# Two attention and feed-forward layers in one decode step: 32 units of K kept instead of 30, and 12 units of streaming room instead of 14

## The chip, the cores and the metric

The kernel runs on one core of a Trainium2 chip. Its time is device microseconds for one launch, the median of three runs: 2575.14 us (2574.99 to 2575.31).

## The reference

Two identical layers (same weights, same K and V caches) are run one after the other on two sequences of one token each, all in float32:

```
x = x + attention(layernorm(x))     # 32 query heads, 8 KV heads, 32768 keys of 128
x = x + geglu(layernorm(x))         # w_gate, w_up 512x1792, w_down 1792x512
x = x + attention(layernorm(x))     # the same K cache, V cache, wq, wo again
x = x + geglu(layernorm(x))
```

`attention` is softmax(q k^T / sqrt(128)) v, then times wo; `geglu` is (gelu(h w_gate) * (h w_up)) w_down. K and V together are 512 MB, and each layer reads all of them.

## The kernel before, in words

**Units and memory.** One unit is 512 float32 columns on 128 partitions, 256 KB. One pair (KV head g, sequence b) has 64 units of K and 64 of V. All that is streamed lies in one tile, `mem`, of 108 units. In the long stretches it holds three pieces of 32 units, K or V, at places 0, 32 and 64; places 96 to 108 hold wo.

**The stream.** Lines 231 to 257 list every transfer in order (wq, K and V of the pairs, wo, then gate and up `gu`, then down `wd`). `pump` issues them on SP's queue in that order; one that has no free place waits and stops all behind it. `done` gives a place back behind the last matmul that reads it, and pumps. So a transfer starts when its place has been read, and it is then queued behind what is still under way. `plan` (line 86) fixes the places of the transfers around the change of layers; the others take the first hole that fits.

**Layer 1 runs the pairs backwards**, so its first pair is the last pair of layer 0. That pair's V (64 units) stays in `mem` and isn't loaded again. Of its K, units 0 to 29 stay in `mem` (`KEPT = 30`: 28 at places 64 to 92, two at 92 and 93), and four more are copied by VectorE and ScalarE into four idle PSUM banks (`stash`, lines 408 to 415) and back later (lines 398 to 403). The other 30 units (34 to 63) are loaded again (`K_PARTS[1]`).

**Between the layers** V and the kept K fill 94 units, and 14 units (places 94 to 108) are left. Through these pass, as a ring of four pieces of 3 to 4 units: `gu` (28 units in 8 pieces), `wd` (14 in 4), wq of layer 1 (32 in 10), the first 14 units of the K that is loaded again. Each is issued when the piece before it at its place has been read. wo of the last head (4 units) is queued between the first and the second piece of the last V and lies at 104; so `gu` piece 3, which takes the same place, is issued only when the last head has been projected (`last_head`, matmuls at line 531).

**The computing chain there**: last V piece (matmuls L457), `combine` (L466, L470, L475), `last_head` (L531), `residual` (L547 to L557), gate and up (L610), gelu, transposed (L584), down (L595 in two pieces, then L531 in two), `residual`, wq (L346), transposed (L358), scores of layer 1 (L386).

Of the kernel before, what the change touches and what calls it, by code (L numbers as in the profile page):

```python
# [16 lines left out]
P = 128  # L17
NB = 2
HKV = 8
REP = 4  # L20
DM = 512
KC = DM // P
DF = 1792
FN = 256
FW = (256, 256, 256, 128)
# [16 lines left out]


K_PARTS = [{ORDER[-1]: [(32, 32), (28, 4), (0, 28)]},
           {ORDER[-1]: [(34, 6), (40, 4), (44, 4), (48, 4), (52, 12)], ORDER[-2]: [(0, 8), (8, 16), (24, 8), (32, 8), (40, 24)]}]

V_SPLIT = [{ORDER[-1]: [32, 16, 8, 4, 4]}, {ORDER[0]: [32, 16, 8, 4, 4]}]


KEPT = 30  # L50
STEPS = [4, 8, 8, 8]


WQ_SPLIT = [[32], [3, 4, 3, 4, 3, 4, 3, 4, 3, 1]]
GU_SPLIT = [[1792, 1792, 1536, 2048], [FH // KC] * KC]
WD_SPLIT = [[3, 4, 3, 4], [3, 4, 4, 2, 1]]

WO_GROUPS = [[(0, 1), (2, 3), (4, 5), (6,), (7,)], [(7,), (6,), (5, 4), (3, 2), (1,), (0,)]]

# [6 lines left out]
def pieces(split):  # L66

    out, s = [], 0
    for n in split:
        out.append((s, n))  # L70
        s += n
    return out
# [13 lines left out]
def plan():  # L86


    last, before = ORDER[-1], ORDER[-2]
    out = {}  # L90

    def put(kind, l, pair, spots):
        for (s, n), o in zip(parts(kind, l, pair), spots):
            out[kind, l, *pair, s] = o

    put("k", 0, before, [32, 0])
    put("v", 0, before, [64, 32])
    put("k", 0, last, [0, SPARE, 64])
    put("v", 0, last, [32, 16, 8, 4, 0])
    out["wo", 0, HKV - 1] = out["wo", 1, HKV - 1] = 104  # L100
    for i in range(8):
        out["gu", 0, i] = [94, 97.5, 101, 104][i % 4]
    for i in range(10):
        out["wd", 0, i] = out["wq", 1, i] = [94, 97, 101, 104][i % 4]
    put("k", 1, last, [98, 104, 94, 64, 68])
    put("k", 1, before, [84, 92, 64, 72, 32])
    put("v", 1, before, [0, 64])
    return out
# [24 lines left out]
def block_kernel(ctx: ExitStack, tc: tile.TileContext, x, consts, kt, vt, wq, wo, won, gu, wd, out):  # L133
# [83 lines left out]
    def flat(src, g, b, s, n):  # L217
        h, c = divmod(s, CHUNK)
        return src[b, g, h, :, c * UNIT:(c + n) * UNIT]

    def add(key, src, rows, cols):
        stream.append((key, src, rows, cols))
# [8 lines left out]
    for l in range(2):  # L231
        for i, (s, m) in enumerate(pieces(WQ_SPLIT[l])):
            add(("wq", l, i), wq[:, s * DM:(s + m) * DM], P, m * DM)
        for n, (g, b) in enumerate(orders[l]):
            second = meets(l, n)[1]
            vp = parts("v", l, (g, b))
            for s, m in parts("k", l, (g, b)):
                add(("k", l, g, b, s), flat(kt, g, b, s, m), P, m * UNIT)
            for s, m in [] if second else vp:
                if n % 2 == 1 and s == vp[1][0]:  # L240
                    group = wo_group(l, g)
                    o = g % 2 * HALF
                    if (l, g) in NARROW:
                        h = NARROW[l, g]
                        add(("won", l, g), won[l, :, :, :h * NSEL * DM], NROW, h * NSEL * DM)
                        add(("wo", l, g), wo[g // 2, :, o + h * DM:o + HALF], P, (REP - h) * DM)
                    elif len(group) == 2 and g == group[0]:
                        add(("wo", l, g), wo[g // 2], P, 2 * HALF)
                    elif len(group) == 1:
                        add(("wo", l, g), wo[g // 2, :, o:o + HALF], P, HALF)  # L250
                add(("v", l, g, b, s), flat(vt, g, b, s, m), P, m * UNIT)
        for e in range(2):
            half_of = gu[e * P * FH:(e + 1) * P * FH].rearrange("(p c) -> p c", p=P)
            for j, (c, m) in enumerate(pieces(GU_SPLIT[l])):
                add(("gu", l, len(GU_SPLIT[l]) * e + j), half_of[:, c:c + m], P, m)
        for j, (o, m) in enumerate(pieces(WD_SPLIT[l])):
            add(("wd", l, j), wd[:, o * DM:(o + m) * DM], P, m * DM)

# [78 lines left out]
    def window(k, v):  # L337
        return xpad[:, 30 + 32 * k - 2 * v:62 + 32 * k - 2 * v]
# [30 lines left out]
    def scores(l, n, g, b):  # L369
        first, second = meets(l, n)  # L370
        mx = wk.tile([P, 2], F32, name="mx", bufs=1)

        todo = [(("k", l, g, b, s), 0, s, m) for s, m in parts("k", l, (g, b))]
        if second:
            own = [(("k", 0, g, b, 0), s, s, m) for s, m in pieces(STEPS)]
            todo = own + [(None, SPARE, KEPT - 2, 2), (None, BACK, KEPT, QUAD)] + todo
        order = [j for key, o, s, m in todo for j in range(s, s + m)]
        for key, o, s, m in todo:
            if key is None:
                w = mem[:, o * UNIT:(o + m) * UNIT].rearrange("p (a c) -> p a c", a=m)  # L380
            else:
                w = get(key, at[key][0][1] if key in at else m)[:, o:o + m, :]
            for j in range(s, s + m):
                u, c, t = j // 32, j // QUAD % 8, j % QUAD
                tile_of = [i for i in order if i // 32 == u and i % QUAD == t]
                nc.tensor.matmul(S[u][32 * t:32 * t + 32, :], qpad[n % 2][:, 28 - 4 * c:60 - 4 * c],  # L386
                                 w[:, j - s, :], start=(j == tile_of[0]), stop=(j == tile_of[-1]))
                if j == [i for i in order if i // 32 == u][-1]:
                    nc.vector.tensor_reduce(mx[:, u:u + 1], S[u], axis=AX.X, op=OP.max)  # L389
            if first and s < KEPT:  # L390
                continue
            if first:

                done(key, 2, m - 2)
            elif key is None:
                give(o, m)
                pump()
            elif second and o + 64 <= BACK < o + m + 64 and key[1] == 0:

                done(key, o, BACK - 64 - o)  # L400
                for bank, i, copy in zip(where, range(QUAD), 2 * [nc.scalar.copy, nc.vector.tensor_copy]):
                    copy(mem[:, (BACK + i) * UNIT:(BACK + i + 1) * UNIT], bank)
                state["full"] = False
            else:
                done(key, o, m)
        return mx

    def stash(g, b):

        places = [SPARE + 2, SPARE + 3, 0, 1]  # L410
        for bank, o, copy in zip(where, places, 2 * [nc.vector.tensor_copy, nc.scalar.copy]):
            copy(bank, mem[:, o * UNIT:(o + 1) * UNIT])
        state["full"] = True
        give(0, 2)
        done(("k", 0, g, b, KEPT - 2), 2, 2)

    def softmax(mx):
        nm = wk.tile([P, 1], F32, name="nm", bufs=1)
# [146 lines left out]
    def feedforward(l):  # L565
# [33 lines left out]

        tops = sum(WD_SPLIT[l][:2])  # L600
        for e in range(2):
            for i, (s, m) in enumerate(pieces(GU_SPLIT[l])):
                key = "gu", l, len(GU_SPLIT[l]) * e + i
                w = flat_of(key)
                c = 0
                for k in range(KC):
                    for t, n in enumerate(FW):
                        if s <= c < s + m:
                            o = both[e][32 * t:32 * t + 32, :].rearrange("p (x c) -> p x c", x=2)[:, :, :n]
                            nc.tensor.matmul(o, window(k, 0), w[:, c - s:c - s + 2 * n].rearrange("p (x c) -> p x c", x=2),  # L610
                                             start=(k == 0), stop=(k == KC - 1))
                        c += 2 * n
                done(key)
                if e == i == 0:
                    spread(A)
                    rstd = state["rstd"]
                    hrr, cube, root = (wk.tile([P, 1], F32, name=n, bufs=1) for n in ("hrr", "cube", "root"))
                    nc.vector.scalar_tensor_tensor(hrr, rstd, 0.5, rstd, op0=OP.mult, op1=OP.mult)
                    nc.vector.tensor_scalar(cube, rstd, math.sqrt(0.044715), None, op0=OP.mult)
                    nc.vector.tensor_scalar(root, rstd, math.sqrt(2.0 / math.pi), None, op0=OP.mult)  # L620
                if e == i == 1:
                    hidden(0)
                if i == len(GU_SPLIT[l]) - 1:
                    gelu(e)
                if e:
                    warm(256, W[:NB])
# [47 lines left out]
def halves(gate, up):  # L674

    out = []
    for e in range(2):
        c, cols = e * DF // 2, []
        for n in FW:
            cols += [gate[:, c:c + n], up[:, c:c + n]]  # L680
            c += n
        w = np.concatenate(cols, axis=1).reshape(KC, P, -1).transpose(1, 0, 2)
        out.append(np.ascontiguousarray(w).reshape(-1))
    return np.concatenate(out)


# [33 lines left out]
```

## Time and profile before

| | |
|---|---|
| median of 3 runs | 2575.14 us |
| the profiled execution | 2575.15 us |
| its span (first to last instruction) | 2573.3 us |
| read from HBM | 1103.71 MB, 429 GB/s over the span |
| TensorE busy, VectorE, ScalarE | 53%, 6%, 3% |
| mean DMA share | 99.5% by queue q1 alone |

Read it from the DMA side: the 16 DMA engines work nearly all the time, and the slices of 64 us that move less than the others are the first, the one around 1300 us (389 GB/s) and the last. The one around 1300 us is the change of layers.

### The profile page before, as it was taken

The numbers are of one execution on the slowest core, as the hardware profiler recorded it, in microseconds if no ns is written. First come the engines' busy times: TensorE is split into PE (matmuls) and PEld (weight loads), VectorE is DVE, ScalarE is ACT, GpSimd is POOL, SyncE is SP. The second block draws the span as 40 slices with busy tenths as digits, with TensorE's granted clock in tenths as the row PEclk, the third lists the DMA queues.
The fourth block names the chain that finished last, engine by engine and source line by source line (L and its number), as shares of the span: only waits on it lengthen the run. The fifth ranks groups of instructions, "written<-read, shape, count | busy, mean of one in ns | idle before, by whom it ended". The sixth has DMA issues, their size and how long they took to land.

```text
span 2573.3 us, 20343 instructions
## 1 busy us (share of the span) xinstructions
PE 1368.5 (53%) x9528; PEld 370.5 (14%) x9528; DVE 143.1 (6%) x482; ACT 80.9 (3%) x187; POOL 2.6 (0%) x10
## 2 busy tenths in 40 slices
PE   3545555445544555564586455454545544554657
PEld 0111111111111111111121111111111111111112
DVE  0000000000000000000011000000000000000001
ACT  0000000000000000000000000000000000000000
POOL 0000000000000000000000000000000000000000
PEclk8777777777777776777798777777777777777779
DMA  9999999999999999999999999999999999999998
GB/s 424 431 432 436 430 431 432 434 432 432 437 427 437 434 426 437 430 431 434 422 389 430 435 434 433 430 434 431 435 430 434 431 433 436 429 436 430 431 435 368
DMA packets 27363, 1105.07 MB, mean 429 GB/s; under 512 B 3184, under 2 KB 3440, under 8 KB 6896
## 3 DMA queue, kind: packets, MB, share of 16 engines
q1 hardware_dynamic: 26992, 1103.70, 99.5%
q8 instruction: 74, 1.21, 0.2%
q10 hardware_dynamic: 288, 0.08, 0.0%
q14 instruction: 9, 0.07, 0.0%
HBM read 1103.71 MB, written 0.07 MB: 429 GB/s over the span
## 4 chain that ended last, share of the span: by engine, by line
DMA 67%; PE 23%; another core or an unknown queue 9%; DVE 1%; ACT 0%; issue 0%; SPq 0%; POOL 0%; ACTq 0%; DVEq 0%
DMA mem<-in_vt 45%; DMA mem<-in_kt 19%; PE A L457 12%; PE S L386 9%; DMA cst<-in_consts 2%; DMA mem<-in_gu 1%; DMA mem<-in_wq 1%; PE W L509 0%; DMA mem<-in_wd 0%; PE M L470 0%; ACT big L466 0%; PE T L432 0%; PE W L491 0%; PE M L346 0%
## 5 line engine op out<-in xcount | busy, mean ns | idle before, releaser
L386 PE MATMUL S<-mem,qpad 128*32 128x512 f32 x4096 | 580.5, 730 | 536.3 <-DMA mem<-in_kt 535.1
L457 PE MATMUL A<-mem,big 128*16 128x512 f32 x4096 | 578.0, 727 | 484.0 <-DMA mem<-in_vt 484.0
L386 PEld LDWEIGHTS S<-mem,qpad 128*32 128x32 f32 x4096 | 146.5, 131 | 957.1 <-issue 512.6
L457 PEld LDWEIGHTS A<-mem,big 128*16 128x16 f32 x4096 | 122.2, 112 | 910.5 <-DMA mem<-in_vt 518.2
L389 DVE TENSOR_REDUCE mx<-S 128x1 f32<-128x512 f32 x64 | 44.3, 692 | 1118.5 <-PE S L386 1118.5
L429 ACT ACTIVATE big<-S,bias 128x512 f32<-128x512 f32 x64 | 43.4, 683 | 1206.6 <-DVE bias L425 1206.6
L432 PE MATMUL T<-cst,big 128*128 128x128 f32 x256 | 50.8, 347 | 39.0 <-ACT big L429 38.7
L475 DVE TENSOR_REDUCE oT<-M 128x4 f32<-128x64 f32 x32 | 7.2, 225 | 1100.6 <-PE M L470 1100.6
L466 ACT ACTIVATE big<-A,linv 128x512 f32<-128x512 f32 (+1 forms) x34 | 22.3, 662 | 1146.9 <-PE A L457 1146.9
L433 DVE COPY big<-T 128x512 f32<-128x512 f32 x64 | 43.8, 691 | 60.8 <-PE T L432 60.8
L432 PEld LDWEIGHTS T<-cst,big 128*128 128x128 f32 x256 | 36.5, 174 | 49.5 <-ACT big L429 49.3
L470 PE MATMUL M<-cst,big 128*128 128x128 f32 x128 | 21.3, 288 | 24.9 <-ACT big L466 24.9
L437 PE MATMUL M<-cst,both 128*128 128x4 f32 x64 | 16.9, 335 | 29.5 <-DVE both L435 29.5
L421 PE MATMUL M<-cst,nm 128*128 128x128 f32 x32 | 10.3, 323 | 34.6 <-DVE nm L419 34.6
L306 PE MATMUL S<-part,cst 128*128 128x128 f32 (+3 forms) x64 | 23.2, 445 | 0.3 <-DVE var L323 0.3
L346 PE MATMUL M<-mem,xpad 128*32 128x512 f32 x128 | 20.1, 637 | 3.9 <-DMA mem<-in_wq 3.4
L470 PEld LDWEIGHTS M<-cst,big 128*128 128x128 f32 x128 | 13.4, 140 | 53.2 <-ACT big L466 53.2
L437 PEld LDWEIGHTS M<-cst,both 128*128 128x128 f32 x64 | 14.1, 275 | 39.4 <-DVE both L435 39.4
L509 PE MATMUL W<-mem,oT 128*2 128x512 f32 x96 | 12.5, 592 | 3.8 <-DVE oT L475 3.8
L421 PEld LDWEIGHTS M<-cst,nm 128*128 128x128 f32 x32 | 4.3, 133 | 63.9 <-DVE nm L419 63.9
L610 PE MATMUL A<-mem,xpad 128*32 128x512 f32 (+1 forms) x64 | 10.2, 623 | 5.5 <-DMA mem<-in_gu 4.3
L491 PE MATMUL W<-mem,big 16*2 16x512 f32 x80 | 12.6, 784 | 0.6 <-DVE big L486 0.6
(100 smaller groups left out, 162.9 us busy)
## 6 DMA issues: line engine op xcount, KB each, us to landing
mem<-in_gu SPq DMA_DIRECT2D x12, 896.0 KB, 24.5
mem<-in_wo SPq DMA_DIRECT2D x5, 2048.0 KB, 53.5
mem<-in_vt SPq DMA_DIRECT2D x2, 4096.0 KB, 42.9
mem<-in_kt SPq DMA_DIRECT2D x1, 7168.0 KB, 49.8
mem<-in_kt SPq DMA_DIRECT2D x3, 2048.0 KB, 16.1
mem<-in_kt SPq DMA_DIRECT2D x1, 6144.0 KB
mem<-in_kt SPq DMA_DIRECT2D x4, 1024.0 KB, 7.7
mem<-in_wo SPq DMA_DIRECT2D x4, 1024.0 KB, 51.0
```

What stands on the lines that cost most here:

```text
L306: nc.tensor.matmul(bank, ident[:, :bank.shape[0]], part.to_broadcast([P, n]), start=True, stop=True)
L346: nc.tensor.matmul(qp[32 * t:32 * t + 32, :], window(k, v), w[:, i - s, :], start=(i < 4), stop=(i >= 8 * KC - 4))
L386: nc.tensor.matmul(S[u][32 * t:32 * t + 32, :], qpad[n % 2][:, 28 - 4 * c:60 - 4 * c], w[:, j - s, :], start=(j == tile_of[0]), stop=(j == ...
L389: nc.vector.tensor_reduce(mx[:, u:u + 1], S[u], axis=AX.X, op=OP.max)
L421: nc.tensor.transpose(m[:, :P], nm.to_broadcast([P, P]), ident)
L429: nc.scalar.activation(p[u], S[u], AF.Exp, bias=bias, scale=SCALE, accum_out=ls[:, u:u + 1])
L432: nc.tensor.transpose(T[u][:, k * P:(k + 1) * P], p[u][:, k * P:(k + 1) * P], ident)
L433: nc.vector.tensor_copy(p[u], T[u])
L437: nc.tensor.matmul(m[:, :REP], both.to_broadcast([P, P]), same, start=True, stop=True)
L457: nc.tensor.matmul(A[32 * t:32 * t + 16, :], p[u][:, at_p:at_p + 16], w[:, QUAD * i + t, :], start=(j == 0), stop=(j == NU // QUAD - 1))
L466: nc.scalar.activation(md[:, i:i + 512 // n], A[:, i:i + 512 // n], AF.Copy, scale=linv)
L470: nc.tensor.transpose(m[:, c * P:(c + 1) * P], md[:, c * P:(c + 1) * P], ident)
```

## The change

Of the last pair's K, 32 units stay in `mem` (places 64 to 96) and units 32 to 35 go through the PSUM banks, so that 28 units (36 to 63) are loaded again instead of 30. For what streams between the layers 12 units are left (places 96 to 108) instead of 14. The pieces become 4 units, some 3 or 2: `gu` 4, 4, 4, 2 and 2, 4, 4, 4 (in both layers; the blocks of a piece are now listed in `GU_PARTS`, the weights lie in HBM in that order, and the matmuls follow it), `wd` of layer 0 3, 4, 4, 3, wq of layer 1 eight times 4, and the K that is loaded again 4, 4, 4, 4, 4, 8. wo of layer 0's last head is queued behind all of the last V, at place 96.

```diff
-           {ORDER[-1]: [(34, 6), (40, 4), (44, 4), (48, 4), (52, 12)], ORDER[-2]: ...
+           {ORDER[-1]: [(36, 4), (40, 4), (44, 4), (48, 4), (52, 4), (56, 8)], ORDER[-2]: ...
-KEPT = 30
-STEPS = [4, 8, 8, 8]
-WQ_SPLIT = [[32], [3, 4, 3, 4, 3, 4, 3, 4, 3, 1]]
-GU_SPLIT = [[1792, 1792, 1536, 2048], [FH // KC] * KC]
+KEPT = 32
+STEPS = [4, 4, 4, 8, 8]
+WQ_SPLIT = [[32], [4] * 8]
+GU_SPLIT = [[2 * sum(FW[t] for k, t in part) for part in parts] for parts in GU_PARTS]
...
-    out["wo", 0, HKV - 1] = out["wo", 1, HKV - 1] = 104
+    out["wo", 0, HKV - 1], out["wo", 1, HKV - 1] = 96, 104
-        out["gu", 0, i] = [94, 97.5, 101, 104][i % 4]
+        out["gu", 0, i] = [100, 104, 96, 100, 102, 104, 96, 100][i]
+        out["wq", 1, i] = [96, 100, 104][i % 3]
+        out["wd", 0, i] = [104, 96, 100, 104][i]
...
-                if n % 2 == 1 and s == vp[1][0]:
+                if n % 2 == 1 and s == vp[1][0] and not meets(l, n)[0]:
...
+            if meets(l, n)[0]:
+                add(("wo", l, g), wo[g // 2, :, g % 2 * HALF:(g % 2 + 1) * HALF], P, HALF)
...
-        places = [SPARE + 2, SPARE + 3, 0, 1]
-        for bank, o, copy in zip(where, places, 2 * [nc.vector.tensor_copy, nc.scalar.copy]):
-            copy(bank, mem[:, o * UNIT:(o + 1) * UNIT])
+        for i, bank, copy in zip(range(QUAD), where, 2 * [nc.vector.tensor_copy, nc.scalar.copy]):
+            copy(bank, mem[:, i * UNIT:(i + 1) * UNIT])
```

SP's queue from the last V of layer 0 (`in_vt` of 16384 columns, then 8192, 4096 and twice 2048) to its `wd`; a unit is 512 columns. Before:

```order
L196 DMA mem<-in_vt 128x16384
L196 DMA mem<-in_wo 128x2048
L196 DMA mem<-in_vt 128x8192
L196 DMA mem<-in_vt 128x4096
L196 DMA mem<-in_vt 128x2048 x2
L196 DMA mem<-in_gu 128x1792 x2
L196 DMA mem<-in_gu 128x1536
L196 DMA mem<-in_gu 128x2048
```

and now:

```order
L203 DMA mem<-in_vt 128x16384
L203 DMA mem<-in_vt 128x8192
L203 DMA mem<-in_vt 128x4096
L203 DMA mem<-in_vt 128x2048 x2
L203 DMA mem<-in_wo 128x2048
L203 DMA mem<-in_gu 128x2048 x3
L203 DMA mem<-in_gu 128x1024 x2
L203 DMA mem<-in_gu 128x2048 x3
```

wo has moved behind the last V piece. Behind that piece there was room for three `gu` pieces, 10.5 units; now there is room for wo and two `gu` pieces, 12 units.

SP's queue from `wd` of layer 0 to the end of the K that layer 1's first pair loads again. Before:

```order
L196 DMA mem<-in_wd 128x1536
L196 DMA mem<-in_wd 128x2048
L196 DMA mem<-in_wq 128x1536
L196 DMA mem<-in_wq 128x512
L196 DMA mem<-in_kt 128x3072
L196 DMA mem<-in_kt 128x2048 x3
L196 DMA mem<-in_kt 128x6144
```

(of `wd` and wq, which alternate 1536 and 2048, two rows each are shown), and now:

```order
L203 DMA mem<-in_wd 128x1536
L203 DMA mem<-in_wd 128x2048 x2
L203 DMA mem<-in_wd 128x1536
L203 DMA mem<-in_wq 128x2048 x8
L203 DMA mem<-in_kt 128x2048 x5
L203 DMA mem<-in_kt 128x4096 x2
```

Ten wq pieces have become eight; of the K, 30 units have become 28 (the last 4096 row belongs to the next pair).

PE's matmuls on the first `gu` half of layer 0. Before:

```order
L610 MATMUL S_87<-mem,xpad 32x512 x3
L610 MATMUL S_87<-mem,xpad 32x2x128
L321 MATMUL A<-sq,part 128x8
L610 MATMUL S_87<-mem,xpad 32x512 x3
L610 MATMUL S_87<-mem,xpad 32x2x128
L610 MATMUL S_87<-mem,xpad 32x512 x3
L610 MATMUL S_87<-mem,xpad 32x2x128
```

and now:

```order
L620 MATMUL S_87<-mem,xpad 32x512 x3
L620 MATMUL S_87<-mem,xpad 32x2x128 x2
L331 MATMUL A<-sq,part 128x8
L620 MATMUL S_87<-mem,xpad 32x512 x6
L620 MATMUL S_87<-mem,xpad 32x2x128 x2
L620 MATMUL S_87<-mem,xpad 32x512 x3
```

The same 16 matmuls of a half, 12 of 512 columns and 4 of 256, stand in another order; a piece has five, four or two of them instead of four.

## Rows read from the trace of the kernel before

**Rows 1.** Page, whole span: its parts 1 to 4
```profile
span 2573.3 us, 20343 instructions
PE 1368.5 (53%) x9528; PEld 370.5 (14%) x9528; DVE 143.1 (6%) x482; ACT 80.9 (3%) x187; POOL 2.6 (0%) x10
...
q1 hardware_dynamic: 26992, 1103.70, 99.5%
q8 instruction: 74, 1.21, 0.2%
...
DMA 67%; PE 23%; another core or an unknown queue 9%; DVE 1%; ACT 0%; issue 0%; SPq 0%; POOL 0%; ACTq 0%; DVEq 0%
```

**Rows 2.** Stretches: busy us (count) by engine, PEclk, DMA share, GB/s
```profile
100.00:1200.00 1100.00, 570.86 (x3910) 150.75 (x3910) 55.61 (x183) 30.49 (x71) 0.00 (x0) 0.73 1.00 432
1285.00:1294.00 9.00, 8.29 (x78) 3.70 (x76) 0.67 (x5) 1.21 (x4) 0.00 (x0) 1.00 0.70 272
1298.00:1302.00 4.00, 1.78 (x10) 0.45 (x10) 1.57 (x4) 0.96 (x2) 0.00 (x0) 0.83 0.95 329
1302.00:1336.00 34.00, 28.14 (x211) 9.20 (x212) 3.03 (x12) 1.95 (x5) 0.55 (x1) 0.97 1.02 420
1336.00:1346.00 10.00, 9.14 (x68) 2.87 (x66) 1.39 (x5) 1.66 (x3) 0.00 (x0) 1.00 1.00 402
1346.00:1360.00 14.00, 7.81 (x68) 2.15 (x64) 1.05 (x2) 0.10 (x1) 0.00 (x0) 0.83 1.02 420
```

**Rows 3.** Chain that ended last, around the last V: start us, us, what
```profile
1261.13 26.88 DMA mem<-in_vt
...
1288.06 1.10 PE A L457 x8
...
1290.82 1.10 PE W L531 x32
...
1291.94 4.81 DMA mem<-in_gu
...
1296.79 1.12 PE S L610 x7
...
1297.92 8.82 DMA mem<-in_gu
```

**Rows 4.** Timeline of SP, 1260 us and 1294 us: start, us, what is issued
```profile
1261.55 30.71 SPq L196 DMA_DIRECT2D mem<-in_gu  x4
1294.36 3.89 SPq L196 DMA_DIRECT2D mem<-in_gu  x4
```

**Rows 5.** Timeline of PE: start, us, out<-in, count, [idle before, releaser]
```profile
1293.24 1.06 PE L610 MATMUL S<-mem,xpad 128*32 128x512 f32 x8
...
1300.22 1.57 PE L610 MATMUL A<-mem,xpad 128*32 128x512 f32 x8 [2.36 <-DMA mem<-in_gu]
...
1306.78 1.07 PE L610 MATMUL A<-mem,xpad 128*32 128x256 f32 x10 [0.34 <-DMA mem<-in_gu]
...
1311.53 1.04 PE L595 MATMUL W<-mem,big 128*2 128x512 f32 x8
...
1333.83 1.07 PE L346 MATMUL M<-mem,xpad 128*32 128x512 f32 x8 [0.80 <-DMA mem<-in_wq]
...
1340.51 4.93 PE L386 MATMUL S<-mem,qpad 128*32 128x512 f32 x44 [0.65 <-DVE qpad L367]
```

**Rows 6.** Copies into the idle banks, line 412: duration ns, first and last start
```profile
L412 ACT COPY T<-mem x1: 590/590/590, 1258.3 to 1258.3; 128x512 f32<-128x512 f32 x1
...
L412 DVE COPY T<-mem x1: 685/685/685, 1260.4 to 1260.4; 128x512 f32<-128x512 f32 x1
```

**Rows 7.** Chain that ended last, the end of the kernel
```profile
2543.72 17.39 DMA mem<-in_gu
...
2561.16 1.11 PE A L610 x2
...
2570.38 0.29 DVE big L562
```

More of the change, by code (lines that the diff above doesn't have):

```diff
@@ L44 @@
 K_PARTS = [{ORDER[-1]: [(32, 32), (28, 4), (0, 28)]},
-           {ORDER[-1]: [(34, 6), (40, 4), (44, 4), (48, 4), (52, 12)], ORDER[-2]: [(0, 8), (8, 16), (24, 8), (32, 8), (40, 24)]}]
+           {ORDER[-1]: [(36, 4), (40, 4), (44, 4), (48, 4), (52, 4), (56, 8)],
+            ORDER[-2]: [(0, 8), (8, 16), (24, 8), (32, 8), (40, 24)]}]
 V_SPLIT = [{ORDER[-1]: [32, 16, 8, 4, 4]}, {ORDER[0]: [32, 16, 8, 4, 4]}]
-KEPT = 30
-STEPS = [4, 8, 8, 8]
-WQ_SPLIT = [[32], [3, 4, 3, 4, 3, 4, 3, 4, 3, 1]]
-GU_SPLIT = [[1792, 1792, 1536, 2048], [FH // KC] * KC]
-WD_SPLIT = [[3, 4, 3, 4], [3, 4, 4, 2, 1]]
+KEPT = 32
+STEPS = [4, 4, 4, 8, 8]
+WQ_SPLIT = [[32], [4] * 8]
+WD_SPLIT = [[3, 4, 4, 3], [3, 4, 4, 2, 1]]
+GU_PARTS = [[[(0, 0), (0, 1), (0, 2), (0, 3), (1, 3)], [(1, 0), (1, 1), (1, 2), (2, 0)],
[3 rows of a table added]
+GU_SPLIT = [[2 * sum(FW[t] for k, t in part) for part in parts] for parts in GU_PARTS]
 WO_GROUPS = [[(0, 1), (2, 3), (4, 5), (6,), (7,)], [(7,), (6,), (5, 4), (3, 2), (1,), (0,)]]
@@ L99, in plan @@
     put("v", 0, last, [32, 16, 8, 4, 0])
-    out["wo", 0, HKV - 1] = out["wo", 1, HKV - 1] = 104
+    out["wo", 0, HKV - 1], out["wo", 1, HKV - 1] = 96, 104
     for i in range(8):
-        out["gu", 0, i] = [94, 97.5, 101, 104][i % 4]
-    for i in range(10):
-        out["wd", 0, i] = out["wq", 1, i] = [94, 97, 101, 104][i % 4]
-    put("k", 1, last, [98, 104, 94, 64, 68])
+        out["gu", 0, i] = [100, 104, 96, 100, 102, 104, 96, 100][i]
+        out["wq", 1, i] = [96, 100, 104][i % 3]
+    for i in range(4):
+        out["wd", 0, i] = [104, 96, 100, 104][i]
+    put("k", 1, last, [104, 96, 100, 64, 68, 72])
     put("k", 1, before, [84, 92, 64, 72, 32])
@@ L251, in block_kernel @@
                 add(("v", l, g, b, s), flat(vt, g, b, s, m), P, m * UNIT)
+            if meets(l, n)[0]:
+                add(("wo", l, g), wo[g // 2, :, g % 2 * HALF:(g % 2 + 1) * HALF], P, HALF)
         for e in range(2):
             half_of = gu[e * P * FH:(e + 1) * P * FH].rearrange("(p c) -> p c", p=P)
-            for j, (c, m) in enumerate(pieces(GU_SPLIT[l])):
-                add(("gu", l, len(GU_SPLIT[l]) * e + j), half_of[:, c:c + m], P, m)
+            for j, (c, m) in enumerate(pieces(GU_SPLIT[e])):
+                add(("gu", l, len(GU_SPLIT[0]) * e + j), half_of[:, c:c + m], P, m)
         for j, (o, m) in enumerate(pieces(WD_SPLIT[l])):
@@ L375, in scores @@
             own = [(("k", 0, g, b, 0), s, s, m) for s, m in pieces(STEPS)]
-            todo = own + [(None, SPARE, KEPT - 2, 2), (None, BACK, KEPT, QUAD)] + todo
+            todo = own + [(None, SPARE, KEPT - QUAD, QUAD), (None, BACK, KEPT, QUAD)] + todo
         order = [j for key, o, s, m in todo for j in range(s, s + m)]
@@ L392, in scores @@
             if first:
-                done(key, 2, m - 2)
+                done(key, QUAD, m - QUAD)
             elif key is None:
@@ L408, in stash @@
     def stash(g, b):
-        places = [SPARE + 2, SPARE + 3, 0, 1]
-        for bank, o, copy in zip(where, places, 2 * [nc.vector.tensor_copy, nc.scalar.copy]):
-            copy(bank, mem[:, o * UNIT:(o + 1) * UNIT])
+        for i, bank, copy in zip(range(QUAD), where, 2 * [nc.vector.tensor_copy, nc.scalar.copy]):
+            copy(bank, mem[:, i * UNIT:(i + 1) * UNIT])
         state["full"] = True
-        give(0, 2)
-        done(("k", 0, g, b, KEPT - 2), 2, 2)
+        give(0, QUAD)
+        pump()
     def softmax(mx):
@@ L601, in feedforward @@
         for e in range(2):
-            for i, (s, m) in enumerate(pieces(GU_SPLIT[l])):
-                key = "gu", l, len(GU_SPLIT[l]) * e + i
+            order = [t for part in GU_PARTS[e] for k, t in part]
+            at_t = 0
+            for i, part in enumerate(GU_PARTS[e]):
+                key = "gu", l, len(GU_PARTS[e]) * e + i
                 w = flat_of(key)
                 c = 0
[L606 to L612, printed above, removed]
+                for k, t in part:
+                    n = FW[t]
+                    o = both[e][32 * t:32 * t + 32, :].rearrange("p (x c) -> p x c", x=2)[:, :, :n]
+                    nc.tensor.matmul(o, window(k, 0), w[:, c:c + 2 * n].rearrange("p (x c) -> p x c", x=2),
+                                     start=(t not in order[:at_t]), stop=(t not in order[at_t + 1:]))
+                    at_t += 1
+                    c += 2 * n
                 done(key)
@@ L622, in feedforward @@
                     hidden(0)
-                if i == len(GU_SPLIT[l]) - 1:
+                if i == len(GU_PARTS[e]) - 1:
                     gelu(e)
@@ L676, in halves @@
     out = []
[L677 to L683, printed above, removed]
+    for e, parts in enumerate(GU_PARTS):
+        cols = []
+        for k, t in sum(parts, []):
+            c = e * DF // 2 + sum(FW[:t])
+            cols += [w[k * P:(k + 1) * P, c:c + FW[t]] for w in (gate, up)]
+        out.append(np.ascontiguousarray(np.concatenate(cols, axis=1)).reshape(-1))
     return np.concatenate(out)
```

3 rows, old and new, of the table GU_PARTS are left out of this document.

## The prediction, written before the changed kernel ran

> **What bounds the kernel now.** The page comes first: TensorE is busy 53% of the span, one DMA queue 99.5%, and the chain that ended last is 67% DMA [rows 1]. In the long stretches data flows at 432 GB/s [rows 2], so a unit of 262,144 bytes takes 0.607 us. Then the stretches around the change of layers: the flow falls to 272 GB/s for 9 us, to 329 for 4 us, and stays at 420 and 402 while the small pieces pass [rows 2]. In work at 432 GB/s that is 9 x (1 - 272/432) = 3.3 us, 0.95 us, 0.9 us and 0.7 us. So a change can gain by moving fewer bytes, or by closing these dips.
>
> Then the chain of waits, to see which dips count. The last V piece landed at 1261.13 + 26.88 = 1288.01; the last head's projection (L531) began 2.81 us behind that and ended 3.9 behind it; it freed the place of gu piece 3, which was issued at 1291.94 and landed at 1296.75 [rows 3]. Between the two landings lie 14.5 units (10.5 that were queued, and these 4). At the full rate they take 8.80 us, and they took 8.74. So the DMA engine that lagged most never ran empty in the 3.3 us dip: what was idle there were engines that had got ahead. As a landing waits for the last engine, this dip cost little by itself. The second dip did cost: piece 4, issued at 1294.36 [rows 4], let its matmuls start at 1300.22 [rows 5]. Its 3.5 units took 3.4 us behind piece 3 instead of 2.1, a loss of 1.3 us.
>
> **Two units less.** 30 units of K loaded again become 28: 2 x 0.607 = -1.21 us, since the stream is the chain before and behind this place. This is the firmest term.
>
> **wo behind V, and 12 units queued in place of 10.5.** V lands 4 units (2.43 us) earlier in the stream, wo 2.43 us behind it. The projection isn't ready to use wo until 2.81 us behind V, so the new wait on wo has 0.4 us in hand. If that were gone, PE's queue behind it (a warming matmul, the residual's, the first gu piece) would come as much later, and the refill that the projection issues with it. The refill is issued 3.9 us behind V as before, with 12 x 0.607 = 7.3 us queued instead of 6.4. I count nothing for this dip alone, by the landings above; 0 to -3.3 us is possible.
>
> **The second dip.** How soon does an issued piece start to land? Piece 3 took 4.81 us for 4 units (2.43), so the lead was 2.38 us [rows 3]. Piece 4 was issued 6.35 us behind V with 14.5 units ahead (8.80 us): 8.80 - 6.35 - 2.38 leaves 0.07 us in hand, and it was late. Now the pieces in its role are the two of 2 units; they wait for the first gu piece, whose matmuls ran from 5.23 to 6.3 us behind V (1293.24 to 1294.3 [rows 5]). Ahead of them lie wo and three pieces, 16 units or 9.7 us: 1.0 us in hand. Of the 1.3 us I take -0.9, as the refills behind are spaced about as before; the bounds are 0 and -1.3.
>
> **A ring of 12 units instead of 14.** When a piece has been read, 8 units are under way in place of about 10.5: 4.86 us instead of 6.4. The reading takes 1.1 us (a wq piece: 1.07 [rows 5]), the lead 2.38: 1.4 us in hand, before 2.9. It is tightest at the first wq piece. It now waits for down's second piece, read until 1311.53 + 1.04 [rows 5], 5.83 us behind the landing of the last gu piece (1297.92 + 8.82 [rows 3]). Under way behind that landing is then only wd, 14 units or 8.50 us: 8.50 - 5.83 - 2.38 = 0.3 us in hand. Before, a wq piece of 3 stood in between, and the piece that waited there had 2.1 us. I cost it at nothing while the 0.3 us hold. The largest lead of the rows is piece 4's, 5.86 - 2.12 = 3.7 us; with that the place would lose 1.1 us, which is the upper end. The lower end is -0.3 us, a third of the 0.9 us that the small pieces lose now, as 3 and 3.5 units grow to 4.
>
> **The K that is loaded again.** Up to the 48th unit its pieces wait for wq reads, those behind for scores. The scores start at 1340.51 [rows 5] in either kernel, and the pieces at 64 and above free as before. The one of 12 becomes 4 and 8, with 20 units ahead of the 8 instead of 18 ahead of the 12, while the piece before has 12 ahead instead of 14. I take 0, within 0.7 us either way (what 402 GB/s lost).
>
> **Copies into the banks.** Four before and four after, on the same engines, the last one from 1260.4 on for 0.69 us [rows 6]. The V piece that waits for them landed 26.88 us after its issue though its own data are 2.4 us, so over 20 us of queued transfers hide it. 0.
>
> **The end.** From the landing of the last gu piece at 2561.12 to the last copy at 2570.38 the chain is computing [rows 7], and wd lies beside it. The last piece now has five matmuls instead of four, two of them in one strip and of half width: 0 to a quarter of the 1.1 us they took, I take +0.1. As the data behind that piece are the same 14 units, this chain moves with the stream and neither hides nor adds to the gain.
>
> **Sum.** -1.21 - 0.9 + 0 + 0 + 0.1 = -2.0 us. The profiled execution took 2575.15 us (span 2573.3 and 1.85 around it), the median of the runs is 2575.14. So 2573.1 us, and 2572.0 to 2574.2 if the forecast's mechanism is right.
>
> **A rule that speaks against the change.** The small pieces of the ring moved at 420 GB/s against 432 [rows 2], 3% less. The Trainium skill ("DMA: Bandwidth & Descriptors", Bandwidth) asks for transfers of 1 MiB or more for 75% of peak. By it the two pieces of 2 units (0.5 MB) in each layer would take at least 1.6 us instead of 1.2, an estimate from that page: 1.6 us in all, and 2574.7 us. The row decides: it holds pieces of 0.75 MB at 97%, since the next transfer is already queued.
>
> **Rivals.**
> - The gain is given back. The two units are saved, but the first wq piece is late by 1.1 us, or the second dip stays: 2574 to 2575.1 us. For it: 0.3 us in hand is little beside leads that range from 2.4 to 3.7 us. Chance 0.2.
> - The first dip counts in full. Then 1.5 more units queued and the even start of all engines behind it give back much of the 3.3 us: 2575.15 - 1.2 - 3.3 = 2570.6 us. For it: 3.3 us of transfers are really missing in [rows 2]. Against it: 8.74 us for 8.80 us of work on the last engine. Chance 0.12.
> - Slower: the ring runs dry on every round. The place is the whole passage from gu to the 48th unit of K, some 27 pieces or 9 rounds of three places. It decides from a lead of 2.38 + 1.4 = 3.8 us on, just above the longest that I can read. At 4.3 us each round would lose 0.5 us: 9 x 0.5 - 1.2 = +3.3 us, 2578.4 us. For it: every refill now depends on a matmul group only two pieces ahead, and any engine that falls behind by more than 1.4 us is felt. Against it: at 10.5 units under way the flow was 420 GB/s with no dip for 34 us [rows 2]. Chance 0.13.
>
> **How the numbers follow.** The forecast has 0.55. The range takes in the best case (2570.6) and, on the other side, the firm -1.2 with the ring's +1.1, K's +0.7 and the end's +0.3: +0.9, or 2576.0 us. Beyond 2576 lies most of the slow rival, below 2570.5 little: 2570.5 to 2576.0 holds some 8 in 10. About what a measurement can tell from no change is 0.2%, here 5.2 us; the forecast lies well within. Faster by more (under 2570.0) only if the first dip counts in full and something else is gained: 0.06. Slower by more (over 2580.3) only if the ring's rounds lose more than 0.7 us each: 0.05. Within: 0.89.
>
> **What would show it.** Read from HBM falls by 0.52 MB. The last V piece lands near 1285.6, the projection starts 2.8 us behind it without waiting for wo, the next gu piece is issued near 1289.5. The stretch of 272 GB/s is shorter by about 1 us, and the dip to 329 is gone. From gu to wq the flow stays near 420, and no matmul of wq waits longer than before for its data. In layer 1 everything lies about 2 us earlier, the last gu piece near 2559.1, and the computing behind it is as long. The prediction is wrong if TensorE waits for data on each third piece of wq (the ring), if the first wq piece lands late, or if the stream behind the passage is earlier by 4 us or more.

## The result, and the profile after

The changed kernel took 2578.26 us (median of 22 runs, 2574.84 to 2581.74) against 2574.99 (median of 22) before: ratio 1.0014, 95% interval 1.0007 to 1.0020. It is 3.3 us slower; 2573.1 us was forecast, 2570.5 to 2576.0 as the range. The time is that of the rival in which the ring runs dry (2578.4 us); its parts are compared below.

The page of the kernel after, its parts 1 and 3, columns as in [rows 1]:

```profile
span 2576.5 us, 20332 instructions
...
q1 hardware_dynamic: 26848, 1103.18, 99.5%
q8 instruction: 74, 1.21, 0.2%
```

The queue moves 0.52 MB less than in [rows 1], the two units, and still the span is 3.2 us longer. The stretches of the kernel after, columns as in [rows 2], show where:

```profile
100.00:1200.00 1100.00, 574.46 (x3910) 150.40 (x3910) 55.58 (x183) 30.50 (x71) 0.00 (x0) 0.72 1.00 432
1285.00:1294.00 9.00, 7.70 (x76) 3.92 (x76) 1.12 (x10) 1.21 (x4) 0.55 (x1) 1.00 0.82 322
1298.00:1302.00 4.00, 2.33 (x13) 0.57 (x14) 1.57 (x4) 0.72 (x2) 0.00 (x0) 1.00 0.97 344
1302.00:1336.00 34.00, 25.74 (x190) 8.39 (x189) 3.03 (x12) 1.95 (x5) 0.55 (x1) 0.90 0.93 354
1320.00:1326.00 6.00, 6.00 (x20) 1.39 (x14) 0.17 (x2) 0.00 (x0) 0.55 (x1) 0.52 0.64 235
1324.00:1325.00 1.00, 1.00 (x3) 0.50 (x2) 0.00 (x0) 0.00 (x0) 0.00 (x0) 0.50 0.00 0
1336.00:1346.00 10.00, 9.07 (x58) 2.65 (x54) 0.46 (x3) 0.69 (x1) 0.00 (x0) 0.83 0.99 372
```

The last column is the one to read. Layer 0 is untouched (432). The dip behind V is shallower (322 for 272). But the 34 us in which gu, wd and wq pass through the ring flow at 354 instead of 420 GB/s, and the next 10 us at 372 instead of 402. In work at 432 GB/s, 34 x (1 - 354/432) = 6.1 us are missing there; before it was 0.9. From 1324 to 1325 us nothing moves at all: the ring has run dry.

The chain of waits of the kernel after, around the change of layers, columns as in [rows 3]:

```profile
1262.45 23.00 DMA mem<-in_vt
...
1288.26 1.10 PE W L540 x32
...
1292.19 5.60 DMA mem<-in_gu
...
1299.01 7.45 DMA mem<-in_gu
...
1312.37 7.27 DMA mem<-in_wq
...
1319.78 1.93 PE M L356 x6
1321.71 0.53 PE S L331 x2
1322.24 1.84 PE M L356 x2
...
1328.21 7.29 DMA mem<-in_wq
```

Start plus duration is a landing, so the rows tell how late the stream is. V landed at 1285.45; each unit behind it should take 0.607 us.

| transfer | units behind V | at full rate | landed | late |
|---|---|---|---|---|
| the second gu piece of 2 units | 20 | 1297.59 | 1297.79 | 0.2 us |
| last gu piece | 32 | 1304.87 | 1306.46 | 1.6 us |
| first wq piece | 50 | 1315.80 | 1319.64 | 3.8 us |
| sixth wq piece | 70 | 1327.94 | 1335.50 | 7.6 us |

TensorE shows it too. Its timeline in the kernel after (start, us, instruction, the idle time before it and what ended that):

```profile
1301.05 1.90 PE L620 MATMUL A<-mem,xpad 128*32 128x512 f32 x8 [1.67 <-DMA mem<-in_gu]
...
1315.64 0.84 PE L540 MATMUL W<-mem,big 128*2 128x128 f32 x24 [0.75 <-DMA mem<-in_wd]
1319.78 1.93 PE L356 MATMUL M<-mem,xpad 128*32 128x512 f32 x6 [1.81 <-DMA mem<-in_wq]
...
1332.09 1.07 PE L356 MATMUL M<-mem,xpad 128*32 128x512 f32 x8 [1.27 <-DMA mem<-in_wq]
1335.54 1.49 PE L356 MATMUL M<-mem,xpad 128*32 128x512 f32 x8 [1.75 <-DMA mem<-in_wq]
```

Before, the longest such waits in wq were 0.8 us [rows 5]. Now they are 1.8. Behind it the granted clock is down to 0.52 on average from 1320 to 1326 (the stretch above), near 1.2 instead of 2.4 GHz, and the first group of the piece takes 1.93 us instead of 1.06. TensorE reads the first wq piece from 1319.78 to 1324.08, in 4.3 us, and the transfer that waits for its place is issued at 1324.11, into the empty queue.

Not all of the 4.3 us is the clock. The first piece has grown from 3 units to 4, and the matmuls of line 331, which follow the third unit, now stand inside it. The ring of 16 below has the same piece and reads it at a clock of 1.00 in 1317.87 + 1.05 - 1316.56 = 2.4 us; the kernel before reads its first piece in 1.06. So 1.3 us come from the new piece and 1.9 from the clock. The end of the kernel after moved with the stream:

```profile
2546.57 17.69 DMA mem<-in_gu
...
2564.30 1.13 PE A L620 x4
...
2573.53 0.29 DVE big L571
```

The last gu piece lands 3.1 us later than in [rows 7], and from there to the last copy it is 9.27 us, before 9.26.

### The profile page after: what moved, and what is told of

Its sections match the earlier page's. It is cut to its first block, busy times and chain, and to the rows that moved or that the text cites. A ratio compares the mean times of both kernels' runs of the same rounds, so it can differ in the third digit from the quotient of the medians.

```text
span 2576.5 us, 20332 instructions
## 1 busy us (share of the span) xinstructions
PE 1379.0 (54%) x9524; PEld 370.8 (14%) x9524; DVE 143.0 (6%) x482; ACT 80.9 (3%) x187; POOL 2.6 (0%) x10
## 3 DMA queue, kind: packets, MB, share of 16 engines
q8 instruction: 74, 1.21, 0.2%
## 4 chain that ended last, share of the span: by engine, by line
DMA 68%; PE 23%; another core or an unknown queue 8%; DVE 0%; ACT 0%; issue 0%; SPq 0%; POOL 0%; ACTq 0%; DVEq 0%
DMA mem<-in_vt 48%; DMA mem<-in_kt 17%; PE A L466 13%; PE S L396 8%; DMA cst<-in_consts 2%; DMA mem<-in_gu 1%; DMA mem<-in_wq 1%; PE M L356 0%; PE W L518 0%; PE M L479 0%; ACT big L475 0%; PE W L500 0%; PE S L316 0%; PE T L441 0%
## 5 line engine op out<-in xcount | busy, mean ns | idle before, releaser
L466 PE MATMUL A<-mem,big 128*16 128x512 f32 x4096 | 588.4, 738 | 479.9 <-DMA mem<-in_vt 479.9
L430 PE MATMUL M<-cst,nm 128*128 128x128 f32 x32 | 10.5, 327 | 34.6 <-DVE nm L428 34.6
```

Of the source, the lines that this page charges most:

```text
L430: nc.tensor.transpose(m[:, :P], nm.to_broadcast([P, P]), ident)
L466: nc.tensor.matmul(A[32 * t:32 * t + 16, :], p[u][:, at_p:at_p + 16], w[:, QUAD * i + t, :], start=(j == 0), stop=(j == NU // QUAD - 1))
```

## The experiments

Each was timed in five rounds against the kernel before, whose medians were 2574.74 us beside the first four, 2575.13 beside the next four, 2574.97 beside the last two. Four suspects were left by the traces: the clock (theory C in the expectations), the new order of wo and the pieces (W), the bytes, and the ring of 12 (D). Later the last was split into pieces that are coarse beside the ring (D1), the ring's size alone (D2) and one late place at the first wq piece (D3).

**Clock held up.** The kernel after, with more warming matmuls around wq in layer 1:

```diff
         qp = small()
+        if l:
+            warm(512)
+            warm(384)
...
             if l:
-                warm(256)
+                warm(512)
```

> The changed kernel with TensorE kept busy: two warming matmuls (512 and 384 columns) ahead of layer 1's first wq piece, where TensorE stood idle for 1.8 us and its granted clock then fell to 0.50, and 512 instead of 256 columns behind each wq piece. Theory C (the loss is the clock: at half clock the first wq pieces are read in 1.9 us instead of 1.06, so the refills behind them are issued 2.5 to 3 us later and all DMA engines run dry): about 2574.5 us, 3 to 4 us below the changed kernel, no stretch at 0 GB/s near 1324 us. Theory D (the ring of 12 units is too shallow by itself, the refill that waits for down's second piece is late at any clock): 2577 to 2578.5 us, the hole stays.

2579.21 us (2576.60 to 2580.74), ratio 1.0016 (1.0007 to 1.0024). Stretches and TensorE's timeline of this kernel, columns as above:

```profile
1320.00:1326.00 6.00, 6.00 (x31) 1.50 (x30) 0.17 (x2) 0.00 (x0) 0.55 (x1) 1.00 0.90 350
1326.00:1336.00 10.00, 7.54 (x40) 1.66 (x32) 0.00 (x0) 0.00 (x0) 0.00 (x0) 1.00 0.99 362
1336.00:1346.00 10.00, 5.72 (x34) 1.57 (x36) 0.46 (x3) 0.69 (x1) 0.00 (x0) 1.00 0.91 320
```
```profile
1329.43 1.06 PE L359 MATMUL M<-mem,xpad 128*32 128x512 f32 x8 [1.81 <-DMA mem<-in_wq]
...
1338.19 1.06 PE L359 MATMUL M<-mem,xpad 128*32 128x512 f32 x8 [1.73 <-DMA mem<-in_wq]
```

The clock is 1.00 throughout and every group takes 1.06 us, yet the waits of 1.8 us come anyway, only later, and the time is no better. So the loss does not need the fallen clock. The test isn't pure: the added warming keeps TensorE about 0.4 us longer between two pieces, which delays releases too, and how much of the loss in the kernel after runs through the clock is not shown.

**Ring of 16.** The kernel after with its new pieces and wo behind V, but 28 units kept and 16 for the ring; 32 units of K are loaded again, four more than in the kernel after:

```diff
-KEPT = 32
+KEPT = 28
...
-        out["wq", 1, i] = [96, 100, 104][i % 3]
+        out["wq", 1, i] = [96, 100, 104, 92][i % 4]
```

> The changed kernel with a ring of 16 units, four places of 4: 28 units of K kept and units 28 to 31 in the banks, 32 units loaded again (4 more than in the changed kernel, 2 more than before); wo stays behind V, the pieces of gu, wd and wq stay. Theory D: the passage loses no more than in the kernel before, about 2576.2 us for the 1.2 us of two more units, and less if the even deeper ring closes dips that the kernel before still has (2574 us). Theory W (the loss comes from wo behind V or from the new pieces and their order): it stays and the bytes come on top, 2580.7 us. Theory C alone gives 2576.2 us as well if TensorE no longer idles ahead of wq.

2572.59 us (2572.30 to 2572.93), ratio 0.9991 (0.9982 to 1.0000). The interval ends at no change, but all 11 runs lie below the lowest of the 33 of the kernel before beside them (2573.78). Four units more to move, and 5.7 us less time than the kernel after. Its stretches, the refills in its chain, and TensorE on the first wq piece:

```profile
1302.00:1336.00 34.00, 26.88 (x213) 9.43 (x213) 3.03 (x12) 2.63 (x6) 0.55 (x1) 1.00 1.01 415
1336.00:1346.00 10.00, 9.35 (x88) 3.09 (x90) 2.44 (x6) 1.07 (x2) 0.00 (x0) 1.00 1.02 424
```
```profile
1296.49 8.76 DMA mem<-in_gu
1306.40 7.53 DMA mem<-in_wd
1314.88 9.00 DMA mem<-in_wq
1325.05 8.77 DMA mem<-in_wq
```
```profile
1316.56 1.06 PE L356 MATMUL M<-mem,xpad 128*32 128x512 f32 x6 [0.26 <-DMA mem<-in_wq]
...
1317.87 1.05 PE L356 MATMUL M<-mem,xpad 128*32 128x512 f32 x2
```

So the pieces of 4, 3 and 2 and the order cost nothing that shows once the ring has 16 units. That they cost nothing in a ring of 12 is not shown by this run; the runs with pieces of 3 below bear on it.

**wo behind V alone.** The kernel before, with only wo moved:

```diff
-                if n % 2 == 1 and s == vp[1][0]:
+                if n % 2 == 1 and s == vp[1][0] and not meets(l, n)[0]:
...
+            if meets(l, n)[0]:
+                add(("wo", l, g), wo[g // 2, :, g % 2 * HALF:(g % 2 + 1) * HALF], P, HALF)
```

> The kernel before with one part of the change: wo of layer 0's last head is queued behind all of the last V, at its old place 104; the ring of 14 units, its pieces and the bytes are those of before. Theory W: slower by some 3 us, 2578 us. Theories D and C: the part is harmless, the first dip (272 GB/s) gets shorter and 2574 to 2575 us.

2572.47 us (2571.76 to 2573.89), ratio 0.9991 (0.9982 to 1.0000): 2.3 us less, and the lowest median of all. Ten of its 11 runs lie below the lowest of the kernel before. Its stretches and the refills in its chain:

```profile
1285.00:1294.00 9.00, 7.37 (x75) 3.49 (x74) 1.12 (x10) 1.21 (x4) 0.55 (x1) 1.00 0.88 348
1298.00:1302.00 4.00, 2.50 (x19) 0.57 (x20) 1.57 (x4) 0.77 (x2) 0.00 (x0) 1.00 1.01 419
1302.00:1336.00 34.00, 28.16 (x210) 9.24 (x208) 3.04 (x12) 1.95 (x5) 0.55 (x1) 1.00 1.02 418
```
```profile
1262.03 23.40 DMA mem<-in_vt
...
1297.73 7.55 DMA mem<-in_gu
1306.46 7.56 DMA mem<-in_wd
1317.72 6.92 DMA mem<-in_wq
1325.79 7.57 DMA mem<-in_wq
```

Here the dip of 329 GB/s at 1298 is closed, as I had expected it of the whole change. By the same sums as in the table above, V landed at 1285.43 and the last gu piece (32 units on) at 1305.28, 0.4 us late; the ninth wq piece (77 units on: 1332.17) landed at 1333.36, 1.2 us late. The kernel after was 7.6 us late at 70 units.

**Two units less alone.** The kernel before with `(52, 10)` for `(52, 12)`; the scores of units 62 and 63 of the last pair in layer 1 are left on old data.

> The kernel before, but units 62 and 63 of the last pair's K are neither loaded nor scored in layer 1 (they are left out of the result), to price two units of transfer by themselves, with the ring of 14 and everything else as before. The prediction's first term: -1.2 us, 2573.8 us. If a transfer less is hidden behind what TensorE does there: 2575.0 us.

2573.41 us (2572.45 to 2575.74), ratio 0.9996 (0.9987 to 1.0005): 1.3 us less. The interval takes in no change, but the size is that of the two units (1.21).

**wo back between the V pieces**, in the kernel after (the edit of the third experiment, undone):

> The changed kernel with wo back between the first and second piece of the last V (still at place 96): one part of the change undone. Behind the last V piece only two gu pieces are then queued, 8 units instead of 12. If wo behind V is what shields the first refill (theory D, and what the run of the old kernel with this one part showed, 2.3 us faster), slower than the changed kernel by 2 to 3 us: 2580.5 us, with a deeper dip between the last V and the third gu piece. If the place of wo doesn't matter once the ring has 12 units: 2578.3 us.

2581.67 us (nine runs, 2578.28 to 2582.99), ratio 1.0025 (1.0015 to 1.0035), 3.4 us over the kernel after. The stretch behind V falls to

```profile
1285.00:1294.00 9.00, 8.35 (x78) 3.83 (x78) 0.67 (x5) 1.21 (x4) 0.00 (x0) 1.00 0.60 226
```

The place of wo is worth 2.3 us at 14 units and 3.4 at 12; with the scatter at 12 units, that it is worth more there is likely, not shown.

**Smaller pieces in the ring of 12.** First wq alone in pieces of 3 at four places, then all that passes the ring (gu, wd, wq, the first K pieces):

```diff
-WQ_SPLIT = [[32], [4] * 8]
+WQ_SPLIT = [[32], [3] * 10 + [2]]
...
-        out["wq", 1, i] = [96, 100, 104][i % 3]
+        out["wq", 1, i] = [96, 99, 102, 105][i % 4]
```

> The changed kernel with layer 1's wq in ten pieces of 3 units and one of 2 at four places instead of eight pieces of 4 at three; the ring stays at 12 units, gu, wd, wo and K as in the changed kernel. Theory D1 (what counts is how much is still under way when a piece has been read, ring less one piece: 9 units now, 8 in the changed kernel): the later wq pieces stop waiting, 2576 us, 2 us below the changed kernel. Theory D2 (what counts is the ring's size alone): 2578.3 us as the changed kernel. Theory D3 (one late place, the first wq piece behind down's second piece, which this doesn't move much): 2578 us.

2576.88 us (2575.05 to 2578.96), ratio 1.0006 (0.9997 to 1.0015), 1.4 less than after, with ranges that overlap: it lies between what D1 (2576) and D2 (2578.3) expect and decides nothing.

> The ring of 12 units and 32 kept units of the changed kernel, but all that streams between the layers in pieces of 3 units at four places (gu 2, 3, 3, 3, 3 and 3, 3, 3, 3, 2; wd 3, 3, 3, 3, 2; wq ten of 3 and one of 2; K four of 3), wo behind V. Under way behind each piece read: 9 units. Theory D1: the passage closes nearly as well as with 14 units, and the two units less are a gain: 2571.5 to 2573.5 us, faster than the kernel before. Theory D2: 2577 to 2578.5 us.

2578.40 us (2575.08 to 2580.70), ratio 1.0013 (1.0004 to 1.0022). No gain, though its profiled execution (2575.4 us) was one of its best. With 9 units under way instead of 8 during a reading I had expected most of the loss back. That coarse pieces are the reason is not borne out. This run also has none of the longer readings of the new pieces: its first wq piece of 3 units isn't cut in two, and no gu piece has two full-width blocks for the same rows of the result (below). So those aren't the reason by themselves either.

**The first wq piece earlier**, in a corner of the ring that is free by then:

```diff
-WD_SPLIT = [[3, 4, 4, 3], ...
-WQ_SPLIT = [[32], [4] * 8]
+WD_SPLIT = [[4, 4, 4, 2], ...
+WQ_SPLIT = [[32], [2] + [4] * 7 + [2]]
```

> The changed kernel with wd in pieces of 4, 4, 4, 2 and wq in 2, seven of 4, 2: the first wq piece (2 units) goes into the corner that wd leaves free and is issued behind down's first piece, and the one that waits for down's second piece has 16 units ahead of it instead of 14. Everything else, and the 8 units under way while wq runs, as in the changed kernel. Theory D3 (the loss is this one place, 0.3 us in hand): the hole near 1324 us goes, 2574.5 to 2575.5 us. Theories D1 and D2 (every refill is too tight): a part of it only, 2577 us or more.

2578.22 us (2577.02 to 2580.91), ratio 1.0012 (1.0003 to 1.0021). The same time as after. From 1320 to 1326 us the flow is 304 GB/s instead of 235, but from 1326 to 1336 it is 338 instead of 385: with that place served early the loss comes at others. It is not one late place.

**The third experiment, its places released later.** The ring has 14 units; what is changed is when TensorE has read a wq piece:

```diff
+                if l and i == s + m - 1:
+                    warm(512)
                 nc.tensor.matmul(qp[32 * t:32 * t + 32, :], window(k, v), w[:, i - s, :],
...
-            if l:
-                warm(256)
```

> The old kernel with wo behind V (2572.5 us) and, in layer 1's wq, a warming matmul of 512 columns ahead of the last matmul of each piece instead of 256 columns behind it: each place of the ring of 14 is read about 1 us later, no byte and no place changes, TensorE's work per piece (1.9 us) stays below the 2.1 us in which a piece lands. Theory D (a refill comes round too late; a place's delay and the ring's size are two sides of one thing: 1 us is 1.6 units of stream, so this is a ring of about 12.4 units while wq runs): part of what the ring of 12 loses comes back as a loss, 2573.5 to 2575.5 us, with TensorE waiting for wq data. If it is the number of units or places as such: 2572.5 us.

2577.44 us (2576.62 to 2579.17), ratio 1.0008 (1.0000 to 1.0017), 5.0 us over the third experiment, more than expected. Stretches and TensorE's timeline:

```profile
1312.00:1320.00 8.00, 7.21 (x93) 3.61 (x88) 0.54 (x5) 0.37 (x2) 0.00 (x0) 1.00 1.02 422
1320.00:1326.00 6.00, 6.00 (x29) 1.35 (x26) 0.00 (x0) 0.00 (x0) 0.55 (x1) 1.00 0.87 311
1326.00:1336.00 10.00, 8.82 (x35) 1.86 (x30) 0.00 (x0) 0.00 (x0) 0.00 (x0) 1.00 0.86 324
```
```profile
1321.72 1.06 PE L350 MATMUL M<-mem,xpad 128*32 128x512 f32 x6
1322.71 1.13 PE L308 MATMUL S<-part,cst 128*128 128x512 f32 x2
1323.77 1.06 PE L350 MATMUL M<-mem,xpad 128*32 128x512 f32 x8
...
1330.10 1.06 PE L350 MATMUL M<-mem,xpad 128*32 128x512 f32 x6 [1.18 <-DMA mem<-in_wq]
```

The flow breaks down at 1320 as in the kernel after, at a clock of 1.00 and with 14 units of ring. But the test is less clean than meant: a piece now holds TensorE for 1323.77 - 1321.72 = 2.05 us, whether it has 3 or 4 units. Without any wait, its matmuls on wq would have followed each other from 1327.87 on, 2.05 us apart, and ended at 1327.87 + 5 x 2.05 + 1.04 = 1339.2; they ended at 1342.1, and in the third experiment at 1336.1. So about half of the delay is TensorE's own work. The other half is the wait for data at 1330.10 and what followed from it. That a later release does harm with 14 units too is made likely by this run, and its size is not shown.

**Ring of 13.** The kernel after with 31 units kept and 13 for the ring, in pieces of 3 and 4:

```diff
-KEPT = 32
+KEPT = 31
...
-        out["wq", 1, i] = [96, 100, 104][i % 3]
+        out["wq", 1, i] = [101, 104, 95, 98][i % 4]
```

> Between the two rings: 31 units of K kept, 29 loaded again, 13 units for what streams between the layers at places of 3, 3, 3 and 4, wo behind V. If the loss sets in with the size of the ring step by step: between the 2572.5 us of 14 units with wo behind V and the 2578.3 us of 12, about 2575 us. If 13 units are still enough, as the larger rings lose almost nothing in the passage: 2571.9 us by the one unit less, which would be the fastest of all.

2573.89 us (2572.74 to 2577.13), ratio 0.9994 (0.9985 to 1.0003), between the neighbours' medians, with a range that overlaps that of 14. Its profiled execution was the slowest of the 11 (2577.13 us), so these stretches show a bad case:

```profile
1320.00:1326.00 6.00, 5.73 (x23) 1.86 (x20) 0.17 (x2) 0.00 (x0) 0.55 (x1) 0.55 0.82 274
1336.00:1346.00 10.00, 8.74 (x64) 2.81 (x62) 0.46 (x3) 0.69 (x1) 0.00 (x0) 1.00 1.03 420
```

With wo behind V, the rings stand like this; the third column adds the units of K saved or spent against the kernel with 14, at 0.607 us each. The pieces differ too: 14 has those of before, 12 and 16 the new ones, 13 its own.

| ring | median | at equal bytes |
|---|---|---|
| 12 (after) | 2578.26 us | 2579.5 |
| 13 | 2573.89 us | 2574.5 |
| 14 (third experiment) | 2572.47 us | 2572.5 |
| 16 | 2572.59 us | 2571.4 |

The kernels with 12 units and wo behind V took 2576.88 to 2578.40 us with four sets of pieces, those with 14 and 16 units 2572.5 and 2572.6 with two: what goes with the loss is the ring, not the pieces.

## Why the prediction was wrong

The step that failed is "A ring of 12 units instead of 14", with its sentence "I cost it at nothing while the 0.3 us hold". By the table it costs 7.0 us (2579.5 - 2572.5): 2574.74 (the kernel before in the rounds of the third experiment) - 2.27 (wo) - 1.21 (two units) + 7.0 gives the 2578.26 us measured. This 7.0 is what is left when the other two parts are taken off, so the sum closes by itself; what bears it out is that the other two parts were run alone, and that rings of 13 and 16 take their places in order.

- **Two units less**, -1.21 us: right in size (-1.3 alone, 0.52 MB less read), though the interval of that run takes in no change.
- **wo behind V**: its mechanism held. The projection began at 1288.26, 2.81 us behind V, and did not wait for wo. V landed at 1285.45 (1285.6 forecast). Its worth was mis-sized: -0.9 us was counted for all that follows from it, and it brings 2.3 us by itself. The first dip, counted at nothing, closes in part, from 272 to 348 GB/s, in that run, the second from 329 to 419; how the 2.3 us divide between the two was not separated. One count was wrong: the three gu pieces queued behind V before have 3.5 + 3.5 + 3 = 10 units, not 10.5. The 8.74 us between the two landings then stand against 14 units or 8.50 us, so that the first dip had cost 0.24 us and not nothing, and piece 4 had been issued 0.2 us too late instead of 0.07 in time.
- **The second dip**, -0.9 us: this gain doesn't show in the kernel after (344 GB/s, and TensorE idle for 1.67 us until 1301.05). The two pieces of 2 units, for which 1.0 us in hand was worked out, were only 0.2 us late. The piece behind them landed 1.0 us late; it was issued at 1294.77, as soon as the second gu piece had been read, and that one, like the piece at 1301.05, takes 1.9 us to read (two of its four blocks go to the same 32 rows of the result), where 1.06 had been taken.
- **The ring.** I took the lead of one refill, 4.81 us for 4 units, as what every refill needs, and found 1.4 us in hand; the reading, 1.1 us, I took from the old pieces, and it is 1.9 us for two of the new gu pieces and 2.4 for the first wq piece at a clock of 1.00. In a stream at full rate a refill's landing lies one ring behind the landing of the piece it replaces. Less the 1.06 us of reading, issue to landing would be 12 x 0.607 - 1.06 = 6.2 us in the ring of 12, 7.4 in that of 14, 8.65 in that of 16. The chains show 7.45 and 7.29 us in the kernel after; 7.55 to 7.57 with 14 in the third experiment from the last gu piece on (one of 6.92); 8.76 to 9.00 with 16, apart from a wd piece of 3 units. With 14 and 16 the refills take what the flow asks for. With 12, these two take 1.1 to 1.2 us too long, and others with 12 still more (9.16 us for one with the clock held up). Each such delay is felt, since the 8 units queued ahead are through by then. The first wq piece shows it by itself: issued at 1312.37 with 14 units of wd ahead, which lay 1312.37 - 1306.46 = 5.9 us behind the last gu piece, it had 8.50 - 5.9 + 2.43 = 5.0 us of data to wait for and took 7.27 us. The 0.3 us in hand became 2.2 us late.
- **The slower rival** was the right mechanism with the wrong size and the wrong chance; that its 2578.4 us meets the measured time is luck. It took 0.5 us for each of 9 rounds of three places; the passage has 23 pieces, less than 8 rounds. The table of landings shows (7.6 - 0.2) us over 50 units, which is 4.2 rounds: 1.8 us each, while before was losing some too. I gave it 0.13 because the flow had held 420 GB/s with 10.5 units under way, which says nothing of 8.
- **The reloaded K, the copies, the end**: no cost shown. The computing behind the last gu piece is 0.01 us longer, +0.1 had been taken.

What is shown is the size of the ring. Open is why a refill with 8 units queued ahead lands over 1 us too late, and with it why pieces of 3 in the ring of 12 gained nothing. The fallen clock delayed single releases, but the kernel with the clock held up took no less time. Packets of the instruction queue (q8, 74 in all) are another candidate that no run took away; between 1312 and 1337 us the kernel after has one of them and those with 14 and 16 units two, so they don't explain the difference by themselves.

The best version found is the kernel before with wo moved (2572.47 us), and nothing of the rest: 2.3 us under the kernel before in the same rounds, 5.8 under the change. The ring of 16 with the new pieces ties with it at 2572.59 us.

## What to carry to other kernels

Memory that feeds a stream just in time can be worth more than the bytes it could save elsewhere, until the refills take what the flow asks for: two units of ring were worth 7 us here, two units of kept data 1.3. Read that from issue-to-landing times of refills under load, compared with ring size over rate less the reading time, and not from the one refill with the shortest lead. Take the reading time of the new pieces, not of the old: cutting them anew can double it. A margin of 0.3 us beside leads that scatter from 2.4 to 3.7 us is no margin, and where the trace shows n units under way to be enough, it has not shown it for fewer.

## What the runs showed of the hardware that was not expected

- The mean flow and the landing of a transfer can tell different things. Before, 272 GB/s over 9 us meant 3.3 us of missing transfers, while the landing behind it was 0.24 us late (8.74 us for 8.50 us of work). That some of the 16 DMA engines had got ahead of the others would fit both numbers; no view here shows the engines one by one.
- Four matmuls of 512 columns for four different groups of 32 rows of the result took 1.06 us, and four of which two go to the same group 1.90 us, both at a granted clock of 1.00 (in the kernel before at 1293.24, in the kernel after at 1301.05).
- A wait of TensorE for data of 1.81 us was followed by a granted clock of 0.52 for 6 us. In the kernel with more warming matmuls, waits of 1.81 and 1.73 us were followed by no fall (1.00 from 1326 to 1346), so the length of one wait does not decide it. The time was the same either way (2578.3 and 2579.2 us).
- The scatter of the runs differs: 2572.30 to 2572.93 us over 11 runs with 16 units, 2574.84 to 2581.74 over 22 with 12.
